# Attention and a squared-ReLU layer on one core: weight chunks converted over two periods, with one order of steps

## The chip, the core and the metric

The kernel runs on one core of a Trainium2 chip. The core has five engines that work side by side: PE (matrix products and transposes), DVE (vector), ACT (scalar functions and copies), POOL (general work on vectors) and SP, which here issues transfers. They wait for each other only through semaphores, and each takes its own instructions strictly in the order in which the program lists them. The metric is the device time of one execution in microseconds (us). The kernel before the change took 1269.42 us (median of 3 runs, 1268.81 to 1269.7).

## The reference

Attention with a threshold, then a feed-forward layer on its output:

```python
scores = scale * np.matmul(q, k.transpose(0, 1, 3, 2))        # q, k, v: (8, 8, 576, 64) float32
thresh = np.max(scores, axis=-1, keepdims=True) - tau
scores = np.where(scores >= thresh, scores, -1000000000.0)
scores = scores - np.max(scores, axis=-1, keepdims=True)
attn = np.exp(scores)
attn = attn / (np.sum(attn, axis=-1, keepdims=True) + 1e-09)
attn_out = np.matmul(attn, v).astype(np.float32)
x = attn_out.transpose(0, 2, 1, 3).reshape(4608, 512)
h = np.maximum(x @ w_in, 0.0)                                 # w_in: (512, 2048)
out = (h * h @ w_out).astype(np.float32)                      # w_out: (2048, 512)
```

The two weight matrices arrive as float64, so the kernel turns them into float32 itself, from the two 32-bit halves of each number.

## The kernel before

**Stages.** The attention stage comes first (to about 494 us of the profile), then the hidden layer, then the output layer. Both layers use sums and differences of weight blocks and of x blocks in place of some of the products (`sums`, `prepare_x`); those of the hidden layer's weights are made on POOL during the attention stage.

**Units and periods.** The 64 pairs of batch and head are taken two heads at a time, in 144 units of 128 query rows. A loop of periods p runs over them; a period starts two units, A = 2p and B = 2p + 1, and finishes older ones, so that the engines have work from several units at once. Period p's work is a table of short steps (`period`, L661): each step issues a few instructions on one engine. A string lists the steps in the order of the program, and a "-" behind a name means the step of the period before, "--" of two before. `step` (L763) makes sure that earlier periods' steps of the same name come first.

**The steps.** On PE: T turns q or k (transposes into banks 1 and 4 of the score memory `sc`, 8 or 10 of them, in 8 periods of 9), SA and SB make the scores of the two units (banks 0, 5 and 2, 3), RA and RB the last 64 keys' scores (banks 1 and 4), V, U and W transpose the softmax weights (V and U into a memory of their own, W into banks 2 and 3), Q spreads the inverse sums beside W, PV multiplies with the values (banks 0 and 5). On ACT: eV, eU, eW and eT copy these results out, powA0 to powB1 are the exponentials, x copies PV's result. On DVE: topA0 to topB1 copy the scores out and find the extreme of each row, maskA0 to maskB1 apply the threshold and sum the row, inv inverts the sums. On POOL: leastA and leastB add tau to the extremes (the masks of that unit need them), over adds 1e-9 to the sums, xm scales x.

**A chunk of weights** (128x512 numbers) is converted by c1 (ACT, the absolute value of the high half), c2 (POOL, the low half to a float), c3 (POOL, limits), c4 and c5 (DVE, shifts and masks of bits), c6 (POOL, adds the two parts). There are 32 chunks, one begun in each of the periods 2 to 33 (`starts`); c1 to c3 run in that period and c4 to c6 in the next. While a chunk is under way the order `CONVERTING` (L628) is used, and x is copied by ACT for both of its halves and scaled on POOL (128x256). From period 35 on the order `PLAIN` (L623) is used: ACT copies one half of x, DVE scales the other half out of `sc`, and POOL scales 128x128. In these periods s1 and s2 make the 44 weight sums, one POOL instruction each, and then those of the first block of x.

**Waits.** `touch` (L378) records who used which bank of `sc`; a later user on another engine waits for the last one of every other engine on that bank. So T of a period waits for topB0 and topB1 of the units before, and the tops wait for the scores.

**Memory.** Raw chunks lie in a ring of 7 buffers at the end of the weight buffer `wall`, the converted parts of c1 in a ring of 6 in `cv`.

Of the kernel before, what the change touches and what calls it, by code (L numbers as in the profile page):

```python
# [48 lines left out]
def kernel(  # L49
# [54 lines left out]
    sb, cv = Region(arena, 0, X_AT[0]), Region(arena, X_AT[0], ARENA)  # L104
# [37 lines left out]
    raw_places = Region(wall, OUTER.index(5) * 7 * BANK, 49 * BANK)  # L142
# [38 lines left out]
    def fetch(m):  # L181
# [7 lines left out]
        raw = raw_places.tile([P, 2 * WC], I32, tag="raw", bufs=7, name="raw")  # L189
# [71 lines left out]
    def sums(W, which, at):  # L261
# [8 lines left out]
        early = which[0:3]  # L270
        for m in (1, 2):
            yield from inner(m, early)
        for op, o, x, y in which:
            for k_ in first:
                to = W[o, k_] if o == y else weight_tile(W, o, k_)
                yield op(nc.gpsimd, to[:, :], W[x, k_][:, :], W[y, k_][:, :])
        for m in OUTER:
            yield from inner(m, which[3:] if m in (1, 2) else which)
# [185 lines left out]
    def softmax(n):  # L464
# [39 lines left out]
        soft[n] = dict(top=top, least=least, power=power, mask=mask, over=over, inverse=inverse)  # L504
# [49 lines left out]
    def values(m):  # L554

        for c in range(CH):
# [56 lines left out]
    def converts(p):  # L613
        return is_wide and (has_chunk(p) or has_chunk(p - 1))

    def has_chunk(p):
        return p in starts

    def begun(n):
# [3 lines left out]
    PLAIN = """  # L623
        put give fetch ahead eU-- powA0-- V-- powA1-- eV-- maskA1-- PV-- powB1-- c1- RA- powB0-- T--
        maskA0-- U- W-- Q-- x-- c4- maskB1-- SA- eT-- RB- maskB0-- topA0- over- topA1- c2 s2 leastA- eW--
        SB- topB0- s1- c5 c6 topB1- inv- leastB- xm-- c3
    """.split()
    CONVERTING = """  # L628
        put give fetch ahead SB- c1 RA topB0- powA1- c2- topB1- PV- c5- powA0- maskA0- eT- leastB- over- V-
        x- T powB0- SA RB W- maskA1- c3 c4 inv- Q- c6- topA0 eV- topA1 leastA U xm- maskB0- powB1- eW- eU  # L630
        maskB1- s1 s2
    """.split()
# [3 lines left out]
        fetch SA RA RB SB topA0 T topA1 leastA topB0 topB1 leastB powA0 powA1 eT more powB0 powB1 maskA0  # L636
        maskA1 maskB0 maskB1
        """.split(),
        1: """
        fetch ahead SA RA RB SB T eT more over topA0 topA1 leastA inv V topB0 topB1 leastB powA0 powA1 eV W  # L640
        Q powB0 eW maskA0 maskA1 powB1 maskB0 maskB1
# [3 lines left out]
    BEGIN_WITH[NU // 2 + 1] = """  # L645
        give eU-- powA0-- V-- powA1-- eV-- maskA1-- PV-- powB1-- powB0-- maskA0-- U- W-- Q-- x--
        maskB1-- maskB0-- eW-- over- inv- eU- xm-- PV- x- V- eV- W- Q- eW- xm- U eU PV x xm
        """.split()

    def spots():  # L650
        return [(sc[:, ds(b * BANK + REST, (FULL + 1) * HALF)], b * BANK) for b in (1, 4)]

# [8 lines left out]
    def period(p):  # L661

        A, B_, a, b = 2 * p, 2 * p + 1, 2 * p - 2, 2 * p - 1
        m, turns = p - 2, TURNS.get(p, ())
# [16 lines left out]
        def W():  # L681
            if has(2 * m + 2):
                pt["W"] = two_banks(w_bank(m + 1))
                fill(m + 1, "W", pt["W"], w_bank(m + 1) * BANK)

        def Q():
            if has(2 * m + 2):
                spread_sums(m + 1, pt["W"], w_bank(m + 1) * BANK)
# [8 lines left out]
        def PV():  # L697
            if has(2 * m):
                values(m)

        def values_out():
            if not has(2 * m):
                return
            late["x"] = x = sb.tile([P, 2, P], FP32, tag="x", bufs=3, name="x")
            for j in range(2):
                from_ = sc[:, ds(5 * j * BANK, P)]
                if converts(p) or j == 0:
                    made = nc.scalar.copy(x[:, j, :], from_)
                else:
                    made = nc.vector.tensor_tensor(  # L710
                        out=x[:, j, :], in0=from_, in1=wT[m][:, ts(SCALE_AT + j, P)], op=ALU.mult
                    )
                touch("x", made, 5 * j * BANK, P, m)

        def given_out():
            if has(2 * m):
                x = late.pop("x")
                made = x[:, 0 : 1 + converts(p), :].rearrange("p j n -> p (j n)")
                scale = wT[m][:, ds(SCALE_AT * P, (1 + converts(p)) * P)]
                nc.gpsimd.tensor_tensor(out=made, in0=made, in1=scale, op=ALU.mult)  # L720
# [697 lines left out]
```

## Time and profile before

The page of the profile tells of one execution of 1273.4 us from the first to the last instruction; the median of the runs is 1269.42 us.

| | PE | DVE | ACT | POOL |
|---|---|---|---|---|
| busy, us | 1251.7 | 988.2 | 844.3 | 982.5 |
| share of the span | 98% | 78% | 66% | 77% |
| busy in 100 to 150 us (conversions) | 48.54 | 49.87 | 49.17 | 46.60 |
| busy in 300 to 350 us (none) | 49.71 | 47.81 | 47.18 | 36.60 |

How to read it: busy time is the time in which an engine had an instruction under way. Matrix products overlap, and their ends are modelled, so a PE that is busy all the time need not be at its fastest. In a timeline row the first number is the start, the second the duration, both in us; then come engine, line, operation, output and input, the count, and in brackets the idle time before it and who ended it. A difference of two starts on one engine is what an instruction costs there, since an instruction's end overlaps with the next one's start. Spans on POOL are rough.

### The profile page before, as it was taken

Reading aid. Unit: us, or ns where it says so; the run is one execution under the profiler, and the core shown is the slowest. Engines: PE = TensorE matmul, PEld = TensorE weight load, DVE = VectorE, ACT = ScalarE, POOL = GpSimd, SP = SyncE. Lnnn points to the kernel's source line nnn. Section 1 sums busy time; section 2 is a strip of 40 time slices with the busy share of each in tenths; the row PEclk is TensorE's granted clock in tenths of the full one; section 3 lists DMA queues with packets and bytes.
Section 4 is the critical chain, followed back from the end, with each engine's and each line's share of the span. In section 5 each row is a group of like instructions: output and inputs, shape, how many; then the busy total and the mean of one; then the engine's idle time right before and its main releaser. Section 6 shows DMA issues by size and latency. Waiting matters only on the chain.

```text
span 1273.4 us, 55161 instructions
## 1 busy us (share of the span) xinstructions
PE 1251.7 (98%) x22991; PEld 1093.6 (86%) x22991; DVE 988.2 (78%) x2385; ACT 844.3 (66%) x1536; POOL 982.5 (77%) x1070
## 2 busy tenths in 40 slices
PE   8999999999999999999999999999999999999998
PEld 5777776777777778988888888999999999999998
DVE  6999998999999996886887878867746654665463
ACT  6999998999999994666765856675524432443240
POOL 2999998877776542988898989868787878787776
PEclk8999999999999999999999999999999999999999
DMA  7566677434333323657667657579965336533511
GB/s 186 143 161 154 167 198 188 120 89 107 89 81 89 83 53 97 192 166 237 202 191 231 215 169 249 172 274 369 267 163 152 83 107 163 146 84 107 167 35 35
DMA packets 289912, 196.79 MB, mean 155 GB/s; under 512 B 98560, under 2 KB 250624, under 8 KB 289664
## 3 DMA queue, kind: packets, MB, share of 16 engines
q1 hardware_dynamic: 288352, 192.86, 52.8%
q8 instruction: 181, 2.97, 1.0%
q14 instruction: 67, 0.55, 0.1%
q10 hardware_dynamic: 1312, 0.41, 0.1%
HBM read 120.85 MB, written 72.35 MB: 152 GB/s over the span
## 4 chain that ended last, share of the span: by engine, by line
PE 72%; DMA 3%; ACT 2%; POOL 2%; DVE 1%; issue 1%; DVEq 0%; ACTq 0%; POOLq 0%; SPq 0%
PE po L818 27%; PE ph L997 17%; PE ph L818 10%; PE sc L561 7%; PE sc L459 6%; PE pt L403 4%; PE sc L542 1%; PE sc L423 1%; POOL arena L126 1%; DMA g<-arena 1%; ACT arena L970 1%; DVE arena L126 1%; DMA w<-arena 1%; ACT arena L971 1%; ACT c L857 1%
## 5 line engine op out<-in xcount | busy, mean ns | idle before, releaser
L126 POOL TENSOR_TENSOR arena<-arena 128x512 f32<-128x512 f32 (+1 forms) x314 | 378.7, 1224 | 125.1 <-DVE arena L126 113.5
L818 PE MATMUL po<-wall,arena 128*64 128x128 f32 x7056 | 385.8, 273 | 1.4 <-ACT arena L813 0.8
L818 PEld LDWEIGHTS po<-wall,arena 128*64 128x64 f32 x7056 | 385.1, 137 | 1.9 <-ACT arena L813 1.0
L126 DVE TENSOR_TENSOR arena<-ph,arena 128x512 f32<-128x512 f32 x378 | 254.5, 688 | 77.4 <-PE ph L997 30.9
L123 POOL TENSOR_TENSOR arena<-arena 128x128 f32<-128x128 f32 (+1 forms) x322 | 265.5, 826 | 24.1 <-DMA arena<-w 8.5
L997 PE MATMUL ph<-arena,wall 128*128 128x256 f32 x1176 | 256.7, 380 | 2.3 <-DVE arena L126 2.1
L997 PEld LDWEIGHTS ph<-arena,wall 128*128 128x128 f32 x1176 | 222.4, 190 | 36.3 <-DVE arena L126 6.2
L126 DVE TENSOR_TENSOR arena<-po,arena 128x128 f32<-128x128 f32 x378 | 107.6, 288 | 159.3 <-PE po L818 151.4
L492 DVE SCALAR_TENSOR_TENSOR arena<-arena 128x576 f32<-128x576 f32 x288 | 225.9, 820 | 0.4 <-ACT arena L487 0.3
L487 ACT ACTIVATE arena<-arena 128x576 f32<-128x576 f32 x288 | 214.1, 781 | 13.4 <-DVE arena L477 13.3
L477 DVE TENSOR_SCALAR_CACHE_REDUCE arena<-sc 128x576 f32<-128x576 f32 x288 | 203.4, 752 | 18.5 <-ACT arena L552 5.7
L857 ACT COPY c<-arena 128x512 f32<-128x512 f32 (+1 forms) x295 | 168.9, 578 | 70.1 <-DVE arena L123 36.1
L459 PE MATMUL sc<-arena 64*64 64x512 f32 (+1 forms) x2304 | 179.6, 415 | 5.6 <-ACT arena L552 1.2
L561 PE MATMUL sc<-arena 64*64 64x128 f32 (+1 forms) x5760 | 165.6, 261 | 1.0 <-ACT arena L552 0.5
L123 DVE TENSOR_TENSOR arena<-arena,c 128x512 f32<-128x512 f32 x235 | 154.2, 664 | 12.1 <-ACT c L857 7.1
L561 PEld LDWEIGHTS sc<-arena 64*64 64x64 f32 x5760 | 150.4, 133 | 4.5 <-ACT arena L552 0.7
L552 ACT COPY arena<-pt 128x1024 f32<-128x1024 f32 x143 | 145.0, 1014 | 4.6 <-PE pt L403 3.9
L459 PEld LDWEIGHTS sc<-arena 64*64 64x64 f32 x2304 | 76.8, 134 | 71.4 <-issue 47.2
L813 ACT COPY arena<-po 128x128 f32<-128x128 f32 x63 | 16.6, 264 | 177.6 <-PE po L818 174.8
L818 PE MATMUL ph<-arena,wall 128*64 128x128 f32 x2352 | 129.2, 273 | 0.6 <-DVE arena L710 0.6
L818 PEld LDWEIGHTS ph<-arena,wall 128*64 128x64 f32 x2352 | 128.3, 137 | 1.4 <-issue 1.0
L484 POOL TENSOR_SCALAR arena<-arena,tau_p 128x2 f32<-128x2 f32 x144 | 83.8, 582 | 58.5 <-DVE arena L477 44.7
(55 smaller groups left out, 1142.5 us busy)
## 6 DMA issues: line engine op xcount, KB each, us to landing
gp<-arena SPq DMA_DIRECT2D x96, 256.0 KB, 3.4
arena<-gp SPq DMA_DIRECT2D x96, 256.0 KB, 5.4
w<-arena SPq DMA_DIRECT2D x60, 256.0 KB, 2.7
wall<-w SPq DMA_DIRECT2D x49, 256.0 KB, 5.3
g<-arena SPq DMA_DIRECT2D x48, 256.0 KB, 3.7
arena<-g SPq DMA_DIRECT2D x48, 256.0 KB, 5.0
arena<-w SPq DMA_DIRECT2D x44, 256.0 KB, 3.4
arena<-in_v_dram SPq DMA_DIRECT2D x32, 288.0 KB, 3.8
```

The source lines that it names most:

```text
L123: e.tensor_tensor(out=out, in0=x, in1=y, op=ALU.subtract)
L126: e.tensor_tensor(out=out, in0=x, in1=y, op=ALU.add)
L459: made = nc.tensor.matmul(sc[at, ds(to, count)], lhs, kT[rows, ds(at_k, count)], start=True, stop=True)
L477: made = nc.vector.tensor_scalar(out=s[:, j, :], in0=sc[:, ds(at, S)], scalar1=1.0, scalar2=None, op0=ALU.mult, op1=ALU.min, accum_out=nmx ...
L484: nc.gpsimd.tensor_scalar(out=thr, in0=nmx, scalar1=tau_p[:, :], scalar2=None, op0=ALU.add)
L487: nc.scalar.activation(out=w[:, :, j, :], in_=of(j), func=AF.Exp, bias=nmx[:, j : j + 1], scale=-1.0)
L492: nc.vector.scalar_tensor_tensor(out=w[:, :, j, :], in0=of(j), scalar=thr[:, j : j + 1], in1=w[:, :, j, :], op0=ALU.is_le, op1=ALU.mult, a ...
L552: touch(kind, copy_by(joined(to), whole(pt, 0, count)), at, 2 * BANK, m)
L561: made = nc.tensor.matmul(sc[ds(u * D, D), ds(5 * j * BANK + row, count)], loaded_v[i][rows, (c - (u != j)) % CH, :], wT[m][rows, ds(weigh ...
L818: nc.tensor.matmul(to[cols], lhs[:, cols], rhs, start=start, stop=stop, skip_group_check=True)
L857: nc.scalar.copy(c, y)
L997: nc.tensor.matmul(to[:, 2 * j : 2 * j + 2, :], W_IN[m, k][:, ts(2 * h + j, P)], part_x(steps, k, m), start=(not more and j == 0), stop=Tr ...
```

## The change

The 32 chunks are begun in every second period (2, 4, ... 64) instead of in 2 to 33. c1 runs in the even period of its start, c3 and c4 in the next (odd) one, c2 and c5 in the even one after that, c6 in the third (odd). One order, `PERIOD`, serves all periods, and `NEEDS` makes a step pull in those that it depends on. Step names are shortened (tA0 for topA0, pA0 for powA0, mA0 for maskA0, lA for leastA). PV is split in PV and P2, x in x0 and x1, and the values of a period's units follow two periods after their scores, not three or four. Until the last two periods, x is copied by ACT for both halves and scaled on POOL (128x256). The weight sums are made in three parts: 6 from period 20, 27 from period 36, 11 behind the attention stage's last periods, with x's sums in between; s1 and s2 issue one each in odd periods. The ring of raw chunks has 4 buffers, further back in `wall`; that of `cv` has 5.

The order of the instructions on the engines in a period p of the changed program, with the period whose step it is:

- PE: T(p), W(p-2), RA(p), RB(p), Q(p-2), SA(p), U(p-2), SB(p), PV(p-2), P2(p-2), V(p-1)
- DVE: mA0(p-1), mB1(p-1), mA1(p-1), tA1(p), tA0(p), mB0(p-1), c4 (odd p) or c5 (even p), tB1(p), tB0(p), inv(p-1)
- ACT: x1(p-3), eV(p-2), c1 (even p), eW(p-2), pB0(p-1), eU(p-2), eT(p), pA0(p), pA1(p), pB1(p), x0(p-2)
- POOL: s1 (odd p), xm(p-3), c3 (odd p), lA(p), over(p-1), c2 (even p), s2 (odd p from 37), lB(p), c6 (odd p), s3 (from 67)

```diff
-    sb, cv = Region(arena, 0, X_AT[0]), Region(arena, X_AT[0], ARENA)
+    sb, cv = Region(arena, 0, X_AT[0]), Region(arena, X_AT[0] + 7 * BANK, ARENA)
...
-    raw_places = Region(wall, OUTER.index(5) * 7 * BANK, 49 * BANK)
+    raw_places = Region(wall, 41 * BANK, 49 * BANK)
...
-        raw = raw_places.tile([P, 2 * WC], I32, tag="raw", bufs=7, name="raw")
+        raw = raw_places.tile([P, 2 * WC], I32, tag="raw", bufs=4, name="raw")
...
-        a = cv.tile([P, WC], I32, tag="a", bufs=6, name="a")
+        a = cv.tile([P, WC], I32, tag="a", bufs=5, name="a")
...
+        five, six, three, seven = which
+
+        def early():
+            for m in (1, 2):
+                yield from inner(m, (five, six, three))
+
+        def middle():
+            yield from outer((five, six, seven))
+            yield from inner(1, (seven,))
+            yield from inner(6, (five, six, three))
+            for m in (7, 4):
+                yield from inner(m, which)
+            yield from inner(5, (five, six, seven))
+
+        def late():
+            yield from outer((three,))
+            for m in (2, 6):
+                yield from inner(m, (seven,))
+            yield from inner(5, (three,))
+            yield from inner(3, which)
+
+        return early(), middle(), late()
...
-    starts = {m + 2: m for m in range(16 + EARLY)}
+    starts = {2 * m + 2: m for m in range(16 + EARLY)}
...
-    summing = deque([sums(W_IN, SUMS_A, AT_A)])
-
-    def sums_due(p):
-
-        return p > max(starts) + 2 and not converts(p)
-
-    def sums_step():
-        while summing and next(summing[0], 0) == 0:
+    LAST_START = max(starts)
+    early, middle, final_ = sums(W_IN, SUMS_A, AT_A)
+    summing = deque([(2 * 7 + 2 + 4, early), (2 * 15 + 2 + 4, middle)])
+
+    def sums_step(p):
+        while summing and p >= summing[0][0]:
+            if next(summing[0][1], 0) != 0:
+                return
             summing.popleft()
...
-    PLAIN = """
-        put give fetch ahead eU-- powA0-- V-- powA1-- eV-- maskA1-- PV-- powB1-- c1- RA- powB0-- T--
-        maskA0-- U- W-- Q-- x-- c4- maskB1-- SA- eT-- RB- maskB0-- topA0- over- topA1- c2 s2 leastA- eW--
-        SB- topB0- s1- c5 c6 topB1- inv- leastB- xm-- c3
-    """.split()
-    CONVERTING = """
-        put give fetch ahead SB- c1 RA topB0- powA1- c2- topB1- PV- c5- powA0- maskA0- eT- leastB- over- V-
-        x- T powB0- SA RB W- maskA1- c3 c4 inv- Q- c6- topA0 eV- topA1 leastA U xm- maskB0- powB1- eW- eU
-        maskB1- s1 s2
-    """.split()
+    PERIOD = """
+        put give fetch ahead mA0- T W-- mB1- RA x1--- RB Q-- eV-- s1--- xm--- SA c1 mA1- tA1 eW-- tA0 c3- pB0- U-- lA eU-- SB eT
+        mB0- PV-- P2-- over- pA0 c4- c5-- c2-- pA1 s2- tB1 tB0 V- lB pB1 c6--- inv- x0-- s3
+    """.split()
+    paced = range(0, LAST_START + 4, 2)
...
+        def scaled_here(j):
+            return p >= NU // 2 - 2
...
-            "s1": lambda: sums_due(p) and sums_step(), "s2": lambda: sums_due(p) and p < 60 and sums_step(), "ahead": lambda: ahead(5), "more": lambda: ahead(7),
-            "fetch": lambda: (fetch(begun(p + 2)), fetch(begun(p + 3)) if p > 1 else None), "put": put, "give": lambda: ask(False),
+            "s1": lambda: p in paced and sums_step(p), "s2": lambda: p in paced and p > 35 and sums_step(p),
+            "s3": lambda: p > LAST_START + 2 and (sums_step(p), sums_step(p)),
+            "ahead": lambda: ahead(5), "more": lambda: ahead(7),
+            "fetch": lambda: [fetch(begun(p + i)) for i in ((2, 3, 4) if p > 1 else (2,))], "put": put, "give": lambda: ask(False),
...
+    NEEDS = {
+        "V": "mA0 mA1 mB0 mB1", "U": "eV", "W": "V", "over": "mA0 mA1 mB0 mB1", "inv": "over", "Q": "W inv",
+        "eV": "V", "eU": "U", "eW": "W Q", "PV": "eV eW", "P2": "PV eU", "x0": "P2", "x1": "P2", "xm": "x0 x1",
+        "eT": "T", "c2": "c1", "c3": "c1", "c4": "c3", "c5": "c4", "c6": "c5 c2",
+    }
...
-                    summing.append(prepare_x(0, lambda op, out, x, y: op(nc.gpsimd, out, x, y)))
+                    prepare = prepare_x(0, lambda op, out, x, y: op(nc.gpsimd, out, x, y))
+                    summing.append((X_FIRST + 6, islice(prepare, 4)))
+                    summing.extend(((LAST_START + 4, prepare), (LAST_START + 4, final_)))
```

More of the change, by code (lines that the diff above doesn't have):

```diff
@@ L1 @@
 from collections import deque
+from itertools import islice
 from contextlib import ExitStack
@@ L268, in inner, with outer @@
                 yield op(nc.gpsimd, to[:, :], W[m, x][:, :], W[m, y][:, :])
[L270 to L278, printed above, removed]
+        def outer(kinds):
+            for op, o, x, y in kinds:
+                for k_ in first:
+                    to = W[o, k_] if o == y else weight_tile(W, o, k_)
+                    yield op(nc.gpsimd, to[:, :], W[x, k_][:, :], W[y, k_][:, :])
+        five, six, three, seven = which
[16 more added lines that the diff above has]
+        return early(), middle(), late()
     later = deque()
@@ L502, in inverse @@
             nc.vector.reciprocal(out=small[:, 3, :], in_=small[:, 2, :])
-        soft[n] = dict(top=top, least=least, power=power, mask=mask, over=over, inverse=inverse)
+        soft[n] = dict(
+            top=top, least=least, power=power, mask=mask, over=over, inverse=inverse
+        )
     def do(n, what, *args):
@@ L552, in filled, with values @@
         touch(kind, copy_by(joined(to), whole(pt, 0, count)), at, 2 * BANK, m)
-    def values(m):
-        for c in range(CH):
+    def values(m, cs):
+        for c in cs:
             for u in range(2):
@@ L753, in period @@
         for letter, n in (("A", A), ("B", B_)):
-            for what, name in (("least", "least"),):
-                steps[what + letter] = lambda n=n, name=name: do(n, name)
-            for what, name in (("top", "top"), ("pow", "power"), ("mask", "mask")):
+            steps["l" + letter] = lambda n=n: do(n, "least")
+            for what, name in (("t", "top"), ("p", "power"), ("m", "mask")):
                 for j in range(2):
@@ L773, in run_period @@
     def run_period(p):
-        for name in BEGIN_WITH.get(p) or (CONVERTING if converts(p) else PLAIN):
+        for name in BEGIN_WITH.get(p) or PERIOD:
             step(name.rstrip("-"), p - name.count("-"))
```

94 lines of the change are left out of this document (50 added, 44 removed).

## The prediction

> **What bounds the kernel now.** I read the page first (span, slices), then the windows view for the two halves of the attention stage, then the timeline engine by engine.
>
> ```profile
> span 1273.4 us, 55161 instructions
> DVE  6999998999999996886887878867746654665463
> ...
> 100.00:150.00 50.00, 48.54 (x1276) 36.28 (x1274) 49.87 (x140) 49.17 (x89) 46.60 (x52) 1.00 0.62 155
> 300.00:350.00 50.00, 49.71 (x1350) 37.13 (x1344) 47.81 (x141) 47.18 (x83) 36.60 (x47) 1.00 0.40 93
> ```
>
> The window columns are busy time of PE, weight load, DVE, ACT, POOL, then PE clock, DMA share and GB/s. In the half with conversions DVE is busy 49.87 of 50 us: DVE sets the pace. In the plain half PE is (49.71), with DVE at 47.81. So all engines are near full, and the pace of a period is what counts. One W eviction (ACT, 128x512) marks each period:
>
> ```profile
> 30.04 0.58 ACT L552 COPY arena<-sc 128x512 f32<-128x512 f32 x1
> ...
> 252.60 0.61 ACT L552 COPY arena<-sc 128x512 f32<-128x512 f32 x1
> ...
> 481.33 0.59 ACT L552 COPY arena<-sc 128x512 f32<-128x512 f32 x1 [0.43 <-PE sc L542]
> ...
> 494.77 5.46 PE L818 MATMUL ph<-arena,wall 128*64 128x128 f32 x96 [0.57 <-DVE arena L710]
> ...
> 505.41 1.28 POOL L126 TENSOR_TENSOR arena<-arena 128x512 f32<-128x512 f32 x1 [10.38 <-DVE arena L126]
> ```
>
> The first is period 3's eviction of W(1), the third that of W(69), beside the last scores. From 30.04 to 252.60 are 32 intervals (6.955 us each, conversions), from there to 481.33 are 36 (6.354, plain): 451.3 us for 68 intervals. This is the term the change works on. The hidden layer starts at 494.77.
>
> What a converting period costs DVE, start to start:
>
> ```profile
> 122.98 1.64 POOL L216 TENSOR_SCALAR wall<-wall 128x512 int32<-128x512 uint32 x1
> ...
> 123.59 0.69 DVE L239 SCALAR_TENSOR_TENSOR wall<-wall,arena 128x512 int32<-128x512 int32 x1
> ...
> 124.19 0.81 DVE L492 SCALAR_TENSOR_TENSOR arena<-arena 128x576 f32<-128x576 f32 x1
> ...
> 124.93 0.81 DVE L492 SCALAR_TENSOR_TENSOR arena<-arena 128x576 f32<-128x576 f32 x1
> ...
> 125.67 0.44 DVE L231 TENSOR_SCALAR arena<-arena 128x512 int32<-128x512 int32 x1
> ...
> 126.03 0.16 DVE L502 RECIPROCAL arena<-arena 128x4 f32<-128x4 f32 x1
> ...
> 126.17 0.76 DVE L477 TENSOR_SCALAR_CACHE_REDUCE arena<-sc 128x576 f32<-128x576 f32 x1
> ...
> 126.85 0.75 DVE L477 TENSOR_SCALAR_CACHE_REDUCE arena<-sc 128x576 f32<-128x576 f32 x1
> ...
> 127.53 0.81 DVE L492 SCALAR_TENSOR_TENSOR arena<-arena 128x576 f32<-128x576 f32 x1
> ```
>
> c5 0.60, a mask 0.74, c4 0.36, inverse 0.14, a top 0.68: 4x0.74 + 4x0.68 + 0.96 + 0.14 = 6.78 us, with no gap.
>
> **The change part by part.** *Conversion over two periods.* DVE loses 0.96 us in every second period's worth: c4 (0.36) falls in odd periods, c5 (0.60) in even ones, for 64 of the 68 intervals. With nothing else in the way DVE needs 2.96 + 2.72 + 0.12 + 0.36 = 6.16 us, or 6.40 in even ones.
>
> *The order on DVE and PE.* After: inverse, mA0, mB1, mA1, tA1, tA0, mB0, c4 or c5, tB1, tB0 on DVE; T, W, rests, Q, SA, U, SB, PV, P2, V on PE. T writes the banks that tB0 and tB1 of the period before have read, and tA1 needs SA: a circle. Its pieces:
>
> ```profile
> 17.84 0.75 DVE L477 TENSOR_SCALAR_CACHE_REDUCE arena<-sc 128x576 f32<-128x576 f32 x1
> 18.65 0.47 PE L403 MATMUL sc<-ident,arena 64*128 64x64 f32 x3 [0.31 <-DVE arena L477]
> ...
> 390.68 0.52 PE L423 MATMUL sc<-ident,arena 64*128 64x64 f32 x10
> 391.04 0.66 PE L403 MATMUL pt<-ident,arena 64*128 64x64 f32 x16
> 391.54 0.29 PE L403 MATMUL sc<-ident,arena 64*128 64x64 f32 x4
> 391.75 0.46 PE L542 MATMUL sc<-ident,arena 64*64 64x64 f32 x16
> 392.04 2.03 PE L459 MATMUL sc<-arena 64*64 64x512 f32 x24
> 394.00 0.27 PE L403 MATMUL pt<-ident,arena 64*128 64x64 f32 x1
> ...
> 393.30 0.76 DVE L477 TENSOR_SCALAR_CACHE_REDUCE arena<-sc 128x576 f32<-128x576 f32 x1 [0.24 <-issue]
> ```
>
> T 0.36, W 0.21, Q 0.29; two SA/SB plus one rest took 1.96, of which I give the rest 0.24, so both rests 0.48. The first top came 1.26 after SA's start, behind one rest; without it I take 1.2. From T to tA1: 2.54. From tA1 on: 1.36 + 0.74 + c + 0.68, then 0.81 from a top's start to the transposes that waited for it (17.84 to 18.65). The circle is 6.49 us with c4, 6.73 with c5.
>
> *mB1 now waits for lB.* This is where I expect the cost. mB1 is the second mask of a period and needs the threshold lB, made on POOL from tB0. Both rows of a least beside masks:
>
> ```profile
> 485.10 0.79 DVE L492 SCALAR_TENSOR_TENSOR arena<-arena 128x576 f32<-128x576 f32 x1
> 485.26 0.78 POOL L484 TENSOR_SCALAR arena<-arena,tau_p 128x2 f32<-128x2 f32 x1 [1.07 <-DVE arena L502]
> ...
> 485.81 0.82 DVE L492 SCALAR_TENSOR_TENSOR arena<-arena 128x576 f32<-128x576 f32 x1
> ```
>
> The mask starts 0.16 earlier, the least ends at 486.04, 0.23 after that mask (485.81), though the next mask already runs. So lB will end 0.23 after mA0 and mB1 starts about 0.24 late: DVE 6.40 and 6.64, as long as the circle. Before, the second mask was not one that waits for this least.
>
> *What POOL does right behind lB.* Its queue is then: even periods c6, xm; odd ones s1 (from period 23, except 35 and 37), xm, c3. c6, s1 and xm have two inputs in SBUF and are ready long before, so one of them meets mB1 and mA1. What such a meeting costs:
>
> ```profile
> 249.62 1.04 POOL L249 TENSOR_TENSOR arena<-wall 128x512 int32<-128x512 int32 x1
> ...
> 250.14 1.14 DVE L492 SCALAR_TENSOR_TENSOR arena<-arena 128x576 f32<-128x576 f32 x1
> ...
> 251.21 0.07 DVE L492 DVE_READ_ACCUMULATOR arena<-arena 128x1 f32 x1
> ...
> 256.94 0.80 DVE L492 SCALAR_TENSOR_TENSOR arena<-arena 128x576 f32<-128x576 f32 x1
> 257.14 1.20 POOL L720 TENSOR_TENSOR arena<-arena 128x256 f32<-128x256 f32 x1
> 257.69 0.07 DVE L492 DVE_READ_ACCUMULATOR arena<-arena 128x1 f32 x1
> 257.69 0.28 DVE L710 TENSOR_TENSOR arena<-sc,arena 128x128 f32<-128x128 f32 x1
> 257.89 1.07 DVE L492 SCALAR_TENSOR_TENSOR arena<-arena 128x576 f32<-128x576 f32 x1
> 258.89 0.08 DVE L492 DVE_READ_ACCUMULATOR arena<-arena 128x1 f32 x1
> ...
> L123 POOL TENSOR_TENSOR wall<-wall 128x512 f32<-128x512 f32 x33 | 42.2, 1278 | 1.5
> ```
>
> The mask at 250.14 took 1.07 to its accumulator, not 0.74: it was held until 250.47, 0.19 before c6's end, so c6 holds 0.85 from its start. xm (L720, 128x256) waited behind the mask of 256.94, and the mask at 257.89 took 1.00, held to 258.15: a waiting xm holds the next mask 0.46 from 257.69. A waiting c6 then costs 0.85-0.08 = 0.77, a waiting s1 1.28-0.19-0.08 = 1.01.
>
> The Trainium skill ("SBUF — State Buffer", Who interferes with whom) states that a DVE instruction with two SBUF inputs contends with a GpSimd instruction that reads SBUF, and that the first to issue has the shared ports for the whole instruction. For c6 and xm the trace agrees (masks of 1.07 and 1.00 against 0.74); for c2 (L216, 122.98 to 124.62) it does not: c5 and the mask at 124.19 kept 0.60 and 0.74 in its time. By the rule alone c2's end would also hold mA0 of every odd period, an estimated 0.2 us x 32, some 6 us more; I go by the rows.
>
> If mB1 gets in first, one waiting operation goes between mB1 and mA1 and xm moves under tA1 and tA0, which do not collide. Even periods: 6.64 + 0.77 = 7.41. Odd with s1 (20): 6.40 + 1.01 = 7.41. Odd without (12): 6.40 + 0.46 = 6.86. Sum 52x7.41 + 12x6.86 = 467.6. The last 4 intervals have no conversion: 6.04 + 0.46, or 1.01 with s1, about 6.7 each, 26.8. Together 494.4 against 451.3: **+43.1 us**. Bounds per collision: 0 (POOL always loses) and both operations ahead of mA1 (below).
>
> *Edits at nothing.* The second x copy and the half abs on ACT: ACT does a whole one of each now in 49.17 of 50 us at 6.78, and gets a longer period. xm of 256 instead of 128 elements is in the above. Moved raw buffers and fetches four periods ahead: loads wait on SP for a c6, with periods of lead; uncovered, the k and q loads behind would stall T by 1 to 2 us a time. The third part of the sums (11 x 1.28 = 14 us) runs under the start of the hidden layer, where POOL idles 10.38 us to 505.41; uncovered, up to 4 us. The drain: the last masks still end it; within 1 us.
>
> **The rivals.** *Both operations first.* If c6 or s1 beats mB1 (POOL starts its next instruction as lB ends) and xm slips in before mA1, then 7.87 (6.64+0.77+0.46, 6.40+1.01+0.46): 52x7.87 + 82.3 + 26.8 = 518.3, +67: 1337. For it: a waiting POOL operation got in at 257.69. Against: mB1 is due within 0.1 us.
>
> *No collision, the circle decides.* If masks always go first: 64x6.61 + 4x6.35 = 448.4, 2.9 less, but PE no longer has cover for stalls like the extra 5.6 us of before's first half (6.955-6.78, 32 times): about 1270, no change. Against: the rows above.
>
> *Faster.* If also lB comes before mA0 and T overlaps better than I take, PE's 6.354 holds throughout: 68x6.354 = 432.1, -19: 1250; halfway to the circle 1260. For it: DVE's bare 6.16 and 6.40. It decides from a mean period below 6.60 us ((451.3-25.4)/64 = 6.65 is break-even).
>
> **How the numbers follow.** The runs' median is 1269.4, 4 us under this execution's span; the difference is put on the median. Forecast 1269.4 + 43 = 1312 us, chance 0.55 (with cases where only some collisions are paid, 1285 to 1325). Both first 0.20, no collision 0.13, faster 0.12. Changes within 0.2% (2.5 us) cannot be told from none: faster 0.15, same 0.05, slower 0.80. The range reaches from below the circle to the double collision: 1264 to 1342; the likeliest case's own is 1285 to 1325.
>
> **What would show it.** Mask rows: mean from 0.81-0.83 us to about 1.0, with mA1 alone at 1.5 to 1.8; a DVE gap near 0.24 before mB1 released by POOL's least; W evictions 7.4 apart in periods 40 to 66 and about 7.1 in 4 to 22; hidden layer starting near 538. Later stages unchanged within 2 us. I am wrong if masks keep 0.74, or if c6 and s1 run beside the tops.

## The result, and the profile after

| | before | after |
|---|---|---|
| time, median of 4 runs | 1269.12 us (1268.26 to 1269.7) | 1372.37 us (1371.29 to 1373.47) |
| profiled execution | 1273.4 us | 1369.5 us |
| from W(1)'s eviction to W(69)'s, 68 intervals | 451.3 us | 547.2 us |
| from there to the end | 792.1 us | 793.8 us |

The changed kernel takes 1.0811 times as long (95% interval 1.0795 to 1.0826). The forecast was 1312 us with a range to 1342, so the sign was right and the size less than half of what came. The two profiled executions differ by 96 us, the medians by 103: the one shown of before was 4 us above its median, the one of after 3 below.

Two rows of the changed kernel's page, then its windows (columns as before: busy PE, weight load, DVE, ACT, POOL), then its timeline at three places (the evictions of W(1) and W(69), and the start of the hidden layer):

```profile
L512 DVE SCALAR_TENSOR_TENSOR arena<-arena 128x576 f32<-128x576 f32 x288 | 316.7, 1118 | 20.1 <-POOL arena L504 18.3
L583 PE MATMUL sc<-arena 64*64 64x128 f32 (+1 forms) x5760 | 167.6, 269 | 101.3 <-DVE arena L497 100.8
```

```profile
100.00:150.00 50.00, 41.29 (x1102) 29.07 (x1104) 47.46 (x116) 41.22 (x75) 31.06 (x36) 1.00 0.41 102
300.00:350.00 50.00, 40.62 (x1062) 28.65 (x1066) 47.44 (x111) 38.98 (x70) 37.81 (x40) 0.97 0.51 140
```

```profile
28.48 0.58 ACT L574 COPY arena<-sc 128x512 f32<-128x512 f32 x1 [1.33 <-PE sc L564]
...
575.72 0.59 ACT L574 COPY arena<-sc 128x512 f32<-128x512 f32 x1
...
592.28 3.93 PE L849 MATMUL ph<-arena,wall 128*64 128x128 f32 x68 [0.72 <-DVE arena L724]
```

DVE is now the busiest engine in both windows (47.4 of 50; time in which a mask is held back counts as busy). PE has fallen to 41 and idles 100.8 us ahead of PV (L583), waiting for tops (L497). The masks' mean went from 820 to 1118 ns. All of the loss lies between the evictions of W(1) and W(69) (547.2 - 451.3 = 95.9 us). The hidden layer starts 16.6 us behind the latter instead of 13.4, and the tail as a whole is 1.7 us longer.

Where the 96 us are on DVE shows in its groups over just these 68 intervals; the last two columns are the idle time ahead of a group and what ended it. Before:

```profile
L492 DVE SCALAR_TENSOR_TENSOR arena<-arena 128x576 f32<-128x576 f32 x273 | 214.4, 820 | 0.0
L477 DVE TENSOR_SCALAR_CACHE_REDUCE arena<-sc 128x576 f32<-128x576 f32 x272 | 192.1, 752 | 15.0 <-ACT arena L552 5.7 <-issue 5.1 <-ACT arena L487 3.5
L710 DVE TENSOR_TENSOR arena<-sc,arena 128x128 f32<-128x128 f32 x36 | 10.1, 280 | 0.0
```

After:

```profile
L512 DVE SCALAR_TENSOR_TENSOR arena<-arena 128x576 f32<-128x576 f32 x272 | 302.7, 1130 | 18.1 <-POOL arena L504 18.1
L497 DVE TENSOR_SCALAR_CACHE_REDUCE arena<-sc 128x576 f32<-128x576 f32 x272 | 194.7, 753 | 11.3 <-DVE arena L512 8.1 <-PE sc L479 2.3 <-ACT arena L574 0.8
```

Masks cost 88.3 us more, the wait for the least (L504) 18.1 more; the waits of the tops cost 3.7 less, the scaling of x on DVE (L710) is gone. 88.3 + 18.1 - 3.7 - 10.1 = 92.6, nearly all of the 95.9 us.

The masks themselves, in an even period (from 301.67) and the odd one behind it. L512 is a mask, L504 a least, L250 is c6, L127 and L124 are sums, L736 is xm, L217 is c2, L497 a top:

```profile
301.67 1.29 POOL L127 TENSOR_TENSOR wall<-wall 128x512 f32<-128x512 f32 x1
302.56 1.01 DVE L512 SCALAR_TENSOR_TENSOR arena<-arena 128x576 f32<-128x576 f32 x1
302.94 0.79 POOL L504 TENSOR_SCALAR arena<-arena,tau_p 128x2 f32<-128x2 f32 x1
303.70 1.03 POOL L250 TENSOR_TENSOR arena<-wall 128x512 int32<-128x512 int32 x1
303.76 1.58 DVE L512 SCALAR_TENSOR_TENSOR arena<-arena 128x576 f32<-128x576 f32 x1 [0.18 <-POOL arena L504]
304.70 1.25 POOL L736 TENSOR_TENSOR arena<-arena 128x256 f32<-128x256 f32 x1
305.28 1.28 DVE L512 SCALAR_TENSOR_TENSOR arena<-arena 128x576 f32<-128x576 f32 x1
306.49 0.08 DVE L512 DVE_READ_ACCUMULATOR arena<-arena 128x1 f32 x1
306.72 0.76 DVE L497 TENSOR_SCALAR_CACHE_REDUCE arena<-sc 128x576 f32<-128x576 f32 x1 [0.15 <-DVE arena L512]
...
309.98 1.62 POOL L217 TENSOR_SCALAR wall<-wall 128x512 int32<-128x512 uint32 x1
310.87 0.79 DVE L512 SCALAR_TENSOR_TENSOR arena<-arena 128x576 f32<-128x576 f32 x1
311.70 0.29 POOL L504 TENSOR_SCALAR arena<-arena,tau_p 128x2 f32<-128x2 f32 x1
311.96 1.28 POOL L127 TENSOR_TENSOR wall<-wall 128x512 f32<-128x512 f32 x1
312.03 1.82 DVE L512 SCALAR_TENSOR_TENSOR arena<-arena 128x576 f32<-128x576 f32 x1 [0.36 <-POOL arena L504]
313.19 1.25 POOL L736 TENSOR_TENSOR arena<-arena 128x256 f32<-128x256 f32 x1
313.78 1.27 DVE L512 SCALAR_TENSOR_TENSOR arena<-arena 128x576 f32<-128x576 f32 x1
```

Read it from 302.94. The least lB ends behind mA0; c6 starts at 303.70 and mB1 at 303.76, 0.06 later: POOL only goes on in its own queue, while DVE waits for POOL's semaphore. mB1 then takes 1.52 us start to start instead of 0.74: c6 held it by 0.78. xm, issued at 304.70 while mB1 ran, gets in ahead of mA1, which takes 1.28 instead of 0.81 (+0.47). In the odd period the sum starts 0.07 ahead of mB1 and holds it to 313.78 (1.75, +1.01); xm again holds mA1. These are the forecast's prices; but two operations are paid in a period, not one. Counted over all 68 intervals, mB1 is held by 54.8 us in all, and mA1 by xm in 53 periods, 24.7 us.

Three smaller things were not in the forecast at all. The first is the sum of s2 that still runs when mA0 starts (302.56: 1.01 against 0.79 at 310.87, +0.22). The second is the 0.15 us ahead of tA1; in front of it the row that reads mA1's accumulator (306.49, 0.08 us) lies open too, which elsewhere runs under the next instruction; the same goes for mA0's in front of the wait for lB. The third is, in odd periods without s1, a hold by c3, an operation with one input (L224; from the same timeline, 0.34 us on the mask of 74.28):

```profile
73.00 0.73 POOL L736 TENSOR_TENSOR arena<-arena 128x256 f32<-128x256 f32 x1
73.07 1.27 DVE L512 SCALAR_TENSOR_TENSOR arena<-arena 128x576 f32<-128x576 f32 x1 [0.36 <-POOL arena L504]
73.70 1.12 POOL L224 TENSOR_SCALAR arena<-arena 128x512 f32<-128x512 f32 x1
74.28 1.15 DVE L512 SCALAR_TENSOR_TENSOR arena<-arena 128x576 f32<-128x576 f32 x1
75.36 0.08 DVE L512 DVE_READ_ACCUMULATOR arena<-arena 128x1 f32 x1
```

### The profile page after: what moved, and what is told of

The parts are those of the page before. It is cut to its first block, busy times and chain, and to the rows that moved or that the text cites. A ratio compares the mean times of both kernels' runs of the same rounds, so it can differ in the third digit from the quotient of the medians.

```text
span 1369.5 us, 55003 instructions
## 1 busy us (share of the span) xinstructions
PE 1253.2 (92%) x22991; PEld 1071.3 (78%) x22991; DVE 1073.1 (78%) x2350; ACT 853.3 (62%) x1571; POOL 1029.0 (75%) x1068
## 3 DMA queue, kind: packets, MB, share of 16 engines
q10 hardware_dynamic: 1312, 0.41, 0.1%
## 4 chain that ended last, share of the span: by engine, by line
PE 60%; DVE 18%; POOL 8%; DMA 5%; issue 4%; ACT 3%; SPq 1%; DVEq 0%; POOLq 0%; ACTq 0%
PE po L849 25%; PE ph L1028 14%; DVE arena L512 10%; PE ph L849 9%; DVE arena L497 6%; PE sc L583 4%; POOL arena L504 4%; PE sc L479 3%; PE pt L423 2%; POOL wall L217 2%; POOL arena L127 1%; DMA arena<-in_k_dram 1%; POOL arena L124 1%; DMA gp<-arena 1%; ACT arena L574 1%
## 5 line engine op out<-in xcount | busy, mean ns | idle before, releaser
L127 POOL TENSOR_TENSOR arena<-arena 128x512 f32<-128x512 f32 (+1 forms) x314 | 378.7, 1224 | 115.8 <-DVE arena L127 101.6
L512 DVE SCALAR_TENSOR_TENSOR arena<-arena 128x576 f32<-128x576 f32 x288 | 316.7, 1118 | 20.1 <-POOL arena L504 18.3
L127 DVE TENSOR_TENSOR arena<-ph,arena 128x512 f32<-128x512 f32 x378 | 254.7, 689 | 77.6 <-PE ph L1028 31.8
L124 POOL TENSOR_TENSOR arena<-arena 128x128 f32<-128x128 f32 (+1 forms) x322 | 267.3, 832 | 23.1 <-DMA arena<-w 7.3
L583 PEld LDWEIGHTS sc<-arena 64*64 64x64 f32 x5760 | 150.9, 138 | 163.1 <-DVE arena L497 161.9
L583 PE MATMUL sc<-arena 64*64 64x128 f32 (+1 forms) x5760 | 167.6, 269 | 101.3 <-DVE arena L497 100.8
L504 POOL TENSOR_SCALAR arena<-arena,tau_p 128x2 f32<-128x2 f32 x144 | 122.8, 852 | 180.9 <-DVE arena L497 152.3
L127 DVE TENSOR_TENSOR arena<-po,arena 128x128 f32<-128x128 f32 x378 | 107.9, 289 | 158.9 <-PE po L849 154.8
L507 ACT ACTIVATE arena<-arena 128x576 f32<-128x576 f32 x288 | 210.7, 783 | 22.5 <-DVE arena L497 22.5
L497 DVE TENSOR_SCALAR_CACHE_REDUCE arena<-sc 128x576 f32<-128x576 f32 x288 | 206.1, 753 | 14.9 <-DVE arena L512 8.2
L479 PE MATMUL sc<-arena 64*64 64x512 f32 (+1 forms) x2304 | 188.5, 419 | 2.2 <-issue 0.8
L124 DVE TENSOR_TENSOR arena<-arena,c 128x512 f32<-128x512 f32 x235 | 154.5, 666 | 10.2 <-ACT c L888 6.1
L423 PEld LDWEIGHTS pt<-ident,arena 64*128 64x128 f32 x2288 | 83.3, 140 | 71.2 <-ACT arena L574 43.0
L844 ACT COPY arena<-po 128x128 f32<-128x128 f32 x63 | 16.6, 264 | 177.5 <-PE po L849 174.8
```

The costliest lines, as they stand in the source:

```text
L124: e.tensor_tensor(out=out, in0=x, in1=y, op=ALU.subtract)
L127: e.tensor_tensor(out=out, in0=x, in1=y, op=ALU.add)
L479: made = nc.tensor.matmul(sc[at, ds(to, count)], lhs, kT[rows, ds(at_k, count)], start=True, stop=True)
L497: made = nc.vector.tensor_scalar(out=s[:, j, :], in0=sc[:, ds(at, S)], scalar1=1.0, scalar2=None, op0=ALU.mult, op1=ALU.min, accum_out=nmx ...
L504: nc.gpsimd.tensor_scalar(out=thr, in0=nmx, scalar1=tau_p[:, :], scalar2=None, op0=ALU.add)
L507: nc.scalar.activation(out=w[:, :, j, :], in_=of(j), func=AF.Exp, bias=nmx[:, j : j + 1], scale=-1.0)
```

## The experiments

The theory (A): POOL's operations behind lB hold DVE's masks, and who has the turn is decided by who starts first. The rivals: the order on PE and DVE (the circle from T to the tops) sets the pace and the masks only fill idle time; or the waits, or the moved buffers. All runs but the last two start from the changed kernel. Each time is that of one execution, but for the last two (medians of four). "Stage" is the time from W(1)'s eviction to W(69)'s, 547.2 us in the changed kernel.

**mB1 behind mA1** (1307.8 us, stage 487.0).

```diff
- mA0- T W-- mB1- RA ... c1 mA1- tA1
+ mA0- T W-- RA ... c1 mA1- mB1- tA1
```

> The changed kernel with one edit: the mask mB1 comes behind mA1 (order mA0, mA1, mB1), all else as it is. Theory A (POOL's operations behind the least lB get in at the next boundary between two masks and hold the mask behind it): mB1 no longer waits for lB (0.24 to 0.36 us gone), one boundary is lost, so that the last operation of the queue (xm in even periods, c3 in odd ones) runs under tA1: 0.46 us less in even and 0.34 in odd periods. About 0.7 us x 64 periods less: 1372 - 45 = about 1327 us; masks' mean falls from 1118 ns to about 1010. Rival B (the circle T, SA, tops on PE and DVE sets the pace, and masks only fill DVE's idle time): the same number of masks lies in the circle, so the time stays at 1372, at most 1372 - 18 = 1354 for the wait. Nothing of the computation is left out.

DVE's groups over its 68 intervals:

```profile
L512 DVE SCALAR_TENSOR_TENSOR arena<-arena 128x576 f32<-128x576 f32 x273 | 270.4, 1016 | 6.1 <-POOL arena L504 6.1
L497 DVE TENSOR_SCALAR_CACHE_REDUCE arena<-sc 128x576 f32<-128x576 f32 x272 | 193.6, 746 | 0.9 <-ACT arena L574 0.5 <-issue 0.2
```

Theory A's side, and 19 us beyond its number. Masks fell by 32.3 us (the lost boundary), the wait for lB by 12.0, the tops' waits by 10.4; this last, the 0.15 us ahead of tA1, was not in the expectation. The rest of the stage's 60 us fits the accumulators' rows that had lain open in front of these waits (11.1 us in all, now 2.8). The rival that the circle sets the pace, which allowed no less than 1354, falls.

**A small operation between lB and c6 or s1** (1343.2 us, stage 520.4). It is 0.22 us on a tile of its own and adds nothing to the result.

```diff
- V- lB pB1 c6--- inv-
+ V- lB wait pB1 c6--- inv-
```

> The changed kernel with one more small operation on POOL (128x4, on a tile of its own, about 0.23 us as over takes) between the least lB and c6 or s1; it adds nothing to the result. In the changed kernel c6 and s1 started 0.06 to 0.07 us ahead of mB1 and held it. Theory A (who starts first after lB has the turn): mB1 is now first, c6 or s1 goes between mB1 and mA1, and the last of the queue (xm in even periods; xm or c3 in odd ones) runs under tA1. That is the forecast's case: 0.46 us less in even, 0.46 or 0.34 in odd periods, 64 x 0.44 = 28 us less: about 1344; mB1 back to 0.74. Rival B (a waiting POOL operation always goes ahead of a mask, whichever started first): the small operation holds mB1 as well, c6 and xm as before: 1372 to 1390.

Its timeline, even period (L784 is the added operation, L250 c6, L736 xm):

```profile
307.87 0.84 DVE L512 SCALAR_TENSOR_TENSOR arena<-arena 128x576 f32<-128x576 f32 x1 [0.20 <-POOL arena L504]
307.92 0.22 POOL L784 TENSOR_SCALAR idle<-idle 128x4 f32<-128x4 f32 x1
308.22 1.39 POOL L250 TENSOR_TENSOR arena<-wall 128x512 int32<-128x512 int32 x1
308.65 1.58 DVE L512 SCALAR_TENSOR_TENSOR arena<-arena 128x576 f32<-128x576 f32 x1
309.58 1.24 POOL L736 TENSOR_TENSOR arena<-arena 128x256 f32<-128x256 f32 x1
310.39 0.76 DVE L497 TENSOR_SCALAR_CACHE_REDUCE arena<-sc 128x576 f32<-128x576 f32 x1 [0.15 <-DVE arena L512]
```

mB1 takes 0.78 start to start, 0.04 more than an unheld mask. c6 starts 0.35 us behind it and holds mA1 instead; xm runs under the tops. This is the order that the forecast had chosen, made true by delaying POOL; the time came within 1 us of the expected 1344. POOL has more to do, and the kernel takes 29 us less. It still takes 31 us more than the forecast's 1312, so the order is not all that the forecast lacked.

**tA0 ahead of tA1** (1356.5 us, stage 531.4).

```diff
- mA1- tA1 eW-- tA0
+ mA1- tA0 eW-- tA1
```

> The changed kernel with tA0 ahead of tA1. DVE idles 0.15 us at tA1, put down to its own mask mA1, which reads the half of the scores' copy that tA1 writes: 8.1 us over the 68 intervals. Theory A: behind mA1 now comes tA0, which writes the other half, so the 0.15 goes: about 1364. Rival B (the wait is for PE's scores, and the name only the nearest event): nothing changes, 1372.

```profile
L497 DVE TENSOR_SCALAR_CACHE_REDUCE arena<-sc 128x576 f32<-128x576 f32 x272 | 193.6, 746 | 1.6 <-ACT arena L574 0.9 <-ACT arena L210 0.4 <-issue 0.2
```

The wait is gone (11.3 to 1.6 in this group, over the same intervals), so it was mA1 and tA1 on one half of a buffer. The stage fell by 15.9 us, 6 more than the wait: the 0.08 us in which mA1's accumulator is read now runs under tA0 (in this run both start at 307.08), which is 68 x 0.08 = 5.4 us.

**POOL's operations in other forms.** In the first of two runs c6, the sums and xm have one input and multiply by 1.0 (1319.4 us, stage 494.7); in the second these and c3 have c2's form (1324.8 us, stage 502.3). Both leave out operands, so their results are not the reference's. The edit of c6 in the second:

```diff
- nc.gpsimd.tensor_tensor(out=a, in0=hi, in1=lo, op=ALU.add)
+ nc.gpsimd.tensor_scalar(out=a, in0=hi.bitcast(U32), scalar1=2.0**-29, scalar2=None, op0=ALU.mult)
```

> The changed kernel with c6, the sums of the attention stage and xm as POOL operations of one input (a multiplication by 1.0 in the form of c3, some 0.67 us for 128x512 before): the second operand is left out, so the weights and the scaling are not the reference's. Theory A1 (it takes two inputs in SBUF on POOL to hold a mask): only c3 can hold one; masks' mean back near 0.82 us, the period at the circle of 6.5 to 6.75 us, 68 x 6.65 = 452 us, time about 1275. Theory A2 (any fast POOL operation that is waiting gets in and holds the mask to 0.19 us before its end, c3 too, as the mask of 1.08 beside c3 suggests): c6 and s1 hold 0.67 - 0.19 - 0.08 = 0.40 instead of 0.77 and 1.01, xm about 0.1 instead of 0.46: 0.7 to 1.0 us less a period, about 1315. Rival B (the circle or the moved buffers, not POOL): stays within 10 us of 1372.

> The changed kernel with c6, c3, the sums of the attention stage and xm all in the form of c2 (one input, unsigned integer to integer, 1.62 us for 128x512, beside which masks kept 0.74 us in the kernel before). The weights and the scaling are not the reference's: the operands and operations are left out. POOL has more to do than in the changed kernel, in the same order and at the same places. Theory A (what costs is that POOL's operations hold DVE's masks): masks' mean near 0.82 us, period at the wait for lB or the circle, 6.5 to 6.75 us: about 1275 us. Rival B (order, circle, waits or moved buffers set the pace): 1372 or more, since POOL's queue gets longer and the least lB later.

The first is near the number of A2, by accident: its operations took 1.50 us, not the 0.67 supposed, and yet held masks by only 0.13 to 0.60. The second lies between its numbers. The masks in the second, where L273 is a sum in c2's form:

```profile
306.48 1.27 DVE L510 SCALAR_TENSOR_TENSOR arena<-arena 128x576 f32<-128x576 f32 x1 [0.34 <-POOL arena L502]
306.52 1.50 POOL L273 TENSOR_SCALAR wall<-wall 128x512 int32<-128x512 uint32 x1
307.67 0.81 DVE L510 SCALAR_TENSOR_TENSOR arena<-arena 128x576 f32<-128x576 f32 x1
308.10 1.09 POOL L734 TENSOR_SCALAR arena<-arena 128x256 int32<-128x256 uint32 x1
```

The 1.50 us operation holds the mask that starts with it by 0.45 (307.67 - 306.48 - 0.74), not by its length, and the next mask runs beside its end at 0.74. c6 in this form held its mask by 0.50 to 0.58. So this form isn't free, as the second expectation had it, and these runs are not runs without holds. What both show: with POOL as busy and its queue in the same order, weaker holds alone take off 48 to 53 us; the rival of order, waits and buffers (1372 or more) falls.

**c4 and c5 behind tB0** (1369.6 us, stage 545.6).

```diff
- pA0 c4- c5-- c2-- pA1 s2- tB1 tB0 V-
+ pA0 c2-- pA1 s2- tB1 tB0 c4- c5-- V-
```

> The changed kernel with DVE's conversion pieces c4 and c5 behind tB0 instead of ahead of tB1. The least lB then has 0.36 to 0.60 us more before mB1 wants it. Theory A: the wait for lB (0.24 in even, 0.36 us in odd periods) goes, the holds stay: 64 x 0.3 = some 19 us less, 1353. Rival B (the circle T, SA, tA1 ... tB0, T sets the pace): c4 and c5 leave the circle, 0.36 + 0.60 us each two periods on top: 64 x 0.48 = 31 us less, 1341 or below. Rival C (an earlier lB lets c6 and s1 start earlier too, which then hold mA0 or c5 as well): no gain, 1372 or more.

```profile
L512 DVE SCALAR_TENSOR_TENSOR arena<-arena 128x576 f32<-128x576 f32 x272 | 297.0, 1117 | 6.4 <-POOL arena L504 6.2 <-issue 0.2
L497 DVE TENSOR_SCALAR_CACHE_REDUCE arena<-sc 128x576 f32<-128x576 f32 x272 | 195.2, 755 | 17.9 <-DVE arena L512 8.1 <-ACT arena L448 5.3 <-PE sc L479 2.4
L232 DVE TENSOR_SCALAR arena<-arena 128x512 int32<-128x512 int32 x32 | 17.2, 536 | 0.0
```

A miss. The wait for lB did fall (18.1 to 6.4), and the masks by some 3.5 (13 ns each), but the tops now wait 6.6 us more, most of it for an ACT copy that PE needs first (L448), c4 takes 3.7 us more than its 13.5, and the rest of the gain is not found in one row. The number is that of rival C, though not by its mechanism: c6 and s1 still held mB1, not mA0 or c5. An earlier least alone is worth next to nothing here.

**POOL's queue reordered**, in four steps: c6 and s1 under the first pair of tops (1358.8 us, stage 536.1); with mB1 behind mA1 too (1322.0, 500.4); with c4 and c5 last too (1293.5, 472.5); without s2 too (1293.2, 460.0). In the first three, and in the last run below, the result is wrong; by the order of the program a sum of x takes the last weight chunk's buffer before it is stored, which was not tried by itself. `over` is split in two (`ov` for the first masks); the other instructions are the same. The first step's edit:

```diff
- eV-- s1--- xm--- SA c1 ... tA0 c3- pB0- U-- lA eU--
+ eV-- SA c1 ... tA0 ov- s1--- c6---- pB0- U-- lA xm--- eU--
- over- pA0 ... lB pB1 c6--- inv-
+ c3- over- pA0 ... lB pB1 inv-
- fetch(begun(p + i)) for i in ((2, 3, 4) if p > 1 else (2,))
+ fetch(begun(p + i)) for i in ((2, 3) if p > 1 else (2,))
```

> The changed kernel with POOL's queue reordered and nothing else on the engines' orders: the addition over is split in two, its first half (A's two columns) waits for mA1; c6 and s1 stand behind that half, so that they run under tA1 and tA0; xm stands behind the least lA, c3 beside the second half of over, c2 and s2 as before. c6 comes half a period later, so the raw weights are fetched three periods ahead instead of four. Theory A (the holds at mB1 and mA1 cost 2.0 to 2.7 us a pair of periods): the holds of c6, s1 and xm go, there stay the waits for lB (0.18 and 0.36), 0.15 us at each tA1 and one hold of c5 by xm (0.46): 12.56 + 0.54 + 0.31 + 0.46 = 13.9 us a pair instead of 16.1: 34 pairs x 2.2 = 75 us less, about 1298. Rival B (order of masks and the circle set the pace, POOL's operations only fill waits): within 10 us of 1372. Nothing is left out.

> POOL's queue as in the run before and the order mA0, mA1, mB1 on DVE; the first part of over covers mA0, mA1 and mB1. Theory A: the two edits touch different terms, so of what is left the waits for lB and the 0.15 us at tA1 go as well: 12.56 + 0.46 = 13.0 us a pair, 68 x 6.5 = 443 against 547 us, about 1268. If the two edits gain the same thing (the mask order alone gained 64 us), nothing more than the better of the two: 1298 to 1308. If the circle of 6.49 and 6.73 us decides, 68 x 6.61 = 449, about 1275.

> As the run before, with c4 and c5 behind tB0, so that xm runs under tB1 and holds nothing, and the pieces leave the circle. Theory A with PE's own pace of 6.354 as the floor: 64 x 6.40 + 4 x 6.35 = 435 us, about 1260, faster than the kernel before. Rival (as where the pieces alone were moved: DVE waits 0.17 us at each first top for PE or ACT, c4 and c5 are held): no gain on the run before, 1270 to 1280. The sums of s2 (periods 37 on, odd) still hold mA0 or mA1 there, about 1 us x 14.

> As the run before, without the second sum of a pair of periods in the attention (s2); those sums run later, behind the last scores. Some 14 sums x 1.28 = 18 us more for POOL after the attention. If the start of the hidden layer has room for them (POOL idles 10.4 us there in the kernel before): 14 us less than the run before in the attention, up to 8 us back behind it: 6 to 14 us faster. If the hidden layer waits for them: 4 us slower.

The first step, over its 68 intervals:

```profile
L512 DVE SCALAR_TENSOR_TENSOR arena<-arena 128x576 f32<-128x576 f32 x272 | 229.5, 862 | 30.5 <-POOL arena L504 30.5
L232 DVE TENSOR_SCALAR arena<-arena 128x512 int32<-128x512 int32 x32 | 13.7, 427 | 46.7 <-POOL arena L224 46.7
```

The holds went as expected (masks 73.2 us less; 75 us of time was expected), yet the time fell by 14: c4 now waits 1.46 us in each odd period for c3, which I had put behind s1, lA and xm, and mB1 waits 12.4 us more for lB. c2 now also starts 0.2 us ahead of mA0 and holds it by 0.27 in 32 periods. The second step still has c4's wait (46.9 us). The third removes it, and a sum of s2 holds mA0 instead (1.04 us at 303.77). The fourth has no such sum:

```profile
L512 DVE SCALAR_TENSOR_TENSOR arena<-arena 128x576 f32<-128x576 f32 x273 | 217.3, 832 | 0.0
L497 DVE TENSOR_SCALAR_CACHE_REDUCE arena<-sc 128x576 f32<-128x576 f32 x272 | 194.6, 752 | 8.9 <-ACT arena L448 5.4 <-ACT arena L574 1.4 <-ACT arena L507 0.5
```

Masks are at 832 ns, near the 820 before the change, and the stage at 460.0 us, 87 less than in the changed kernel; but the sums left out of it come behind, and the rest takes 804.0 us (1291.4 - 487.4) instead of the third step's 792.2. Not every hold is gone, though: c2 starts beside c5 and holds it (0.94 us against 0.70 in the changed kernel), 7.4 us over its 32. The first three steps came out 34 to 61 us above theory A's numbers, each by a new wait or a hold moved elsewhere. The fourth, expected 6 to 14 us faster than the third, was as long: 12.5 us less in the stage, 11.8 more behind it.

**c3 in even periods, c2 behind lB**, from the fourth step, without s2 and with it: 1298.8 us (stage 465.6; 1.0221 times before, 1.0202 to 1.0239) and 1300.0 us (478.4; 1.0229, 1.0203 to 1.0254).

```diff
- lA xm--- eU-- ... c3- over- pA0 c2-- pA1 ... lB pB1
+ lA xm--- c3 eU-- ... over- pA0 pA1 ... lB c2-- pB1
```

> From the run with POOL's queue, mask order and pieces moved and without s2: c3 comes in even periods behind xm (c4, in the odd period behind, no longer waits for it) and c2 right behind the least lB, where it starts within mA1. No operation of two inputs on POOL stands ahead of a mask any more. Theory A: masks' mean at 0.82, DVE's pair near 12.6 to 12.9 us with PE's own 12.7 beside it: 34 x 12.9 = 439 us for the 68 intervals, instead of 460; with the 804 us behind them (the late sums cost 11) and 27 ahead 1270, the median 1272: as long as the kernel before. Rival (c2 behind lB holds mB1 by 0.41 to 0.48 as operations of its form did): 34 x 0.45 = 15 us more, 1287.

> As the run before with s2 in odd periods from 39 on, behind xm and over, under the last top. Theory A: s2 starts about 1.1 us into the 1.36 us of the tops and c4 (0.36), so it holds mA0 by about 0.5 to 0.9 us in 14 periods, 7 to 13 us, and takes 11 us of late sums away from behind the attention: 1270, within 6 us of the run before either way. Rival (late sums do not matter): 7 to 13 us slower than the run before.

```profile
311.75 0.79 DVE L512 SCALAR_TENSOR_TENSOR arena<-arena 128x576 f32<-128x576 f32 x1
311.98 2.10 POOL L217 TENSOR_SCALAR wall<-wall 128x512 int32<-128x512 uint32 x1
312.46 1.26 DVE L512 SCALAR_TENSOR_TENSOR arena<-arena 128x576 f32<-128x576 f32 x1
313.66 0.81 DVE L512 SCALAR_TENSOR_TENSOR arena<-arena 128x576 f32<-128x576 f32 x1
```

The first is a miss, 6 us slower than the fourth step. Its rival named the right hold, at another mask: c2, issued within mA0, waits to its end (2.10 us instead of 1.60), gets in ahead of mA1 and holds it by 0.46. The tops' waits grew to 12.5 us besides, so the time lies 12 us above even the rival's 1287. The second is as long as the first within their intervals. Its s2 held c4, not mA0 (at 380.59: 1.52 us instead of 0.42), and that cost about what the later sums did. No arrangement tried is as fast as the kernel before.

## What the prediction had right, and the step that failed

**DVE sets the pace: right.** DVE is busy 47.4 of 50 us in both halves, and what was taken off DVE came off the time wherever no new wait took its place. The conversion's pieces fell one to a period, as said.

**The wait for lB: right.** 0.18 us in even periods and 0.36 in odd ones, where c2 makes lB late, against 0.24 in each; 18.1 us in all against 68 x 0.24 = 16.3.

**The prices of a hold: right.** 0.78, 1.01 and 0.47 us against 0.77, 1.01 and 0.46.

**"If mB1 gets in first, one waiting operation goes between mB1 and mA1": the step that failed.** mB1 didn't get in first: POOL starts its next operation 0.06 to 0.07 us before DVE, which waits for the semaphore. The row that I weighed against it, "mB1 is due within 0.1 us", was the very row that decided: being due 0.06 us later loses the turn. So both operations hold a mask in nearly every period. The rival named for this, "both operations first", with a chance of 0.20, was the right mechanism. The run with the small operation is the test: with c6 0.35 us behind mB1's start instead of 0.06 ahead, the chosen order appears, and 29 us go. Of the signs named, the gap before mB1 came as said; the mask of 1.5 to 1.8 us was mB1 (1.58 and 1.82), not mA1.

**What the sum lacked.** The stage took 547.2 us, 96 over before, where 43 were forecast. Held time, the masks' mean over 0.81 us: 272 x (1.130 - 0.81) = 87.0, against 53.0 in the forecast (32 x 0.77 + 20 x 1.01 + 12 x 0.46 = 50.4, and 26.8 - 4 x 6.04 = 2.6 in the last four intervals): 34.0 more. Of these, the second holds by xm are 24.7, c3's 3.8 and those of sums beside mA0 and mA1 4.5. Waits of the tops: 11.3, against nothing. The wait for lB: 1.8 more. The rest of DVE, 547.2 - 87.0 - 18.1 - 11.3 = 430.8 against 425.1 (64 x 6.28 + 4 x 5.80, without waits or holds): 5.7 more. The accumulators' rows that lie open in front of the two waits more than cover this: the sum counted each mask at 0.74, as if its accumulator were always read under the next instruction; over the stage 11.1 us of such rows lie open, against 2.6 before. 34.0 + 11.3 + 1.8 + 5.7 = 52.8 = 95.9 - 43.1. That is also why the right rival's 1337 was 35 us short: it had the second hold of xm, and none of the others. In the run with the small operation the masks are held by 57.7 us, near the forecast's 53.0, and what it still takes more are the waits of the tops (11.9), open rows (10.9) and the wait for lB (18.8). The remaining 7 us of the miss lie between the profiled executions and the medians.

**What stood at nothing.** c3 is named in POOL's queue behind xm but has no price; it holds a mask where there is no s1. mA1 right ahead of tA1 shares a buffer with it, which no term covers. The late sums and the drain were right: 1.7 us in the tail, the forecast's bound being 2; and no wait of DVE or PE in the stage names a transfer. The circle of 6.49 and 6.73 us was never reached, so its size stays open; tops' waits of 8.9 and 12.5 us in the fourth reordering and the run behind it, at 6.76 and 6.85 us a period, may mean that it is near, which was not tried.

**The rule that I set aside.** The Trainium skill ("SBUF — State Buffer", Who interferes with whom) has the first to issue keep the shared ports for its whole instruction, whatever the operation on POOL, as long as it reads SBUF. The forecast let it go for c2. At 310.87 the mask beside c2's end took 0.79 us, unheld, so the estimate drawn from it (6 us more) is not borne out; but the same form holds a mask by 0.45 when it starts beside it, and c3 by 0.34, so the row I went by (122.98) was not the whole of it either. On the first to issue having the turn, the runs agree with the page where the rows lie clearly apart (0.35 us in the run with the small operation); at 306.48 the mask's row starts 0.04 us ahead of POOL's, and the mask is held all the same, so rows this close do not tell who came first. In both cases the turn went to POOL, which had no semaphore to wait for.

## What to carry to other kernels

When a mask waits for a result of the engine it contends with, ask what that engine does in the next tenth of a microsecond: here its queue went on 0.06 us before DVE did, so the operation behind the result went first. Put such operations where the other engine does not collide with them (here under the tops, which read `sc` and kept their 0.75 us), and count what each move makes late: four reorderings here took off most of the holds and won back only 14 to 79 us of 103, because each left something else waiting.

## What the runs showed of the hardware

- An operation of one input in c2's form holds a mask only at its start: by 0.45 to 0.58 us when both start together, out of 1.50 to 1.60, and not at all beside its end (0.79 at 310.87). One with two inputs holds it to 0.19 before its end.
- Multiplying 128x512 float32 by 1.0 on POOL took 1.50 us; c3, with a minimum and a maximum over as many elements, 0.61 where nothing held it (means of one run, the first of the two with other forms).
- Small operations are held too. A least takes 0.29 us where no mask runs (lB at 311.70). lA took 1.05 and 1.31 us beside mB0 with c4 or c5 behind it (at 300.23 and 308.27 in the changed kernel), ending 0.06 to 0.07 us behind both. The least at 485.26 in the kernel before took 0.78 and got in behind one mask. Why it waits for two instructions there and for one here was not tried.
